# One square root batch for the first two chunks, and another hand-written order of every queue

## The chip, the cores and the metric

The kernel runs on one core of a Trainium2 chip. The metric is the time of one execution on the device in microseconds; several executions are made and their median is taken.

## The reference

Two layers in a row, on x of shape (4, 6336, 256), that is 25344 tokens of 256 features:

```python
# first layer: a gated linear recurrence over the tokens of each batch
a_t  = exp(8 * sigmoid(r_gate) * log(clip(sigmoid(a_param))))
norm = sqrt(max(1 - a_t * a_t, 1e-6))
x_gated = norm * sigmoid(i_gate) * x
for t in range(S):
    h = a_t[:, t] * h + x_gated[:, t]
    y[:, t] = h
# second layer, on y: a causal convolution of 5 taps per feature makes a gate
gate = sigmoid(sum_k conv_w[k] * shifted(y, k))
out  = (gate * (y @ w_val)) @ w_out
```

All inputs and the output are float32 in device memory: r, i and x are read (78 MB) and the output is written (26 MB).

## The kernel before

The tokens are cut into 51 *windows* of 256 or 512 tokens, and the windows into 28 *chunks*: chunk 0 and 1 are one window of 256 each, chunk 2 one of 512, chunks 3 to 25 two windows of 512 each, chunk 26 one of 512, chunk 27 one of 256. So chunk c from 3 on holds windows 2c-3 and 2c-2. Every step is a small function `op_xx`, and the list `ORDER` names the steps one after the other with their chunk or window (and half h of the 256 features), and after an @ the PSUM banks. Each engine takes its own instructions in the order of that list; a step waits on its engine until its inputs are there and its buffer is free, and everything later on that engine waits behind it. No scheduler moves anything.

The life of a chunk, by the names of the steps:

- `lr`, `li`, `lx` (w): SyncE issues the load of a window's r, i or x into rings of four windows each (`NRI`, `NII`, `NX`), so a load of window w can only be issued when the window four earlier has been read. All loads and all stores stand in the one queue of SyncE.
- `ta` (c), `tb` (c): ScalarE, tanh of r/2 and of i/2 (the sigmoids). `pp`, `up` (w): GpSimd, tanh + 1, then times x; for windows 1, 2 and 6 TensorE brings x into PSUM (`xp`) and VectorE does both (`uv`).
- `tr` (c, h): TensorE transposes the tanh of r, `ex` (c, h): ScalarE takes the exponential into `aring` (the decay a, features on the partitions; chunks paired by `GROUPS`). `sq` (c, h): GpSimd squares a (`sa`: ScalarE does).
- `rt` (b): ScalarE takes sqrt(0.25 - 0.25 a^2) over all chunks of batch b of `BATCHES`, into `ering`. The square root needs another table than tanh and exp, so going there and back costs two table loads (line 529).
- `nt` (c): TensorE transposes the roots, `xg` (c): VectorE multiplies them into u, `xt` (c): TensorE transposes the product, `sc` (c, h): VectorE runs the recurrence as one scan per half into `yring`.
- `cv` (w): TensorE convolution, `tg`: ScalarE tanh of it, `vl`: TensorE y @ w_val, `gv`: VectorE product of the two, `ou`: TensorE product with w_out, `cd` or `ca`: copy of the result from PSUM to `oring` (four slots, `NOSB`) by VectorE or by ScalarE, `st`: SyncE issues the store.
- `s_wl` (k): the four loads of the weights, `s_wcast`: GpSimd casts them.

The lines of the profile: L188 and L529 table loads, L289 loads, L307 ta, L310 tb, L317 pp, L329 up, L334 xp, L343 uv, L354 tr, L370 ex, L378 sq, L397 rt, L412 nt, L419 xg, L428 xt, L450 sc, L462 cv, L469 tg, L477 vl, L482 gv, L492 ou, L500 cd, L502 ca, L513 st.

Two places that words don't give as well, the root over a batch, and the walk over the list with its table loads:

```python
            while k < len(cs):
                m = k + 1
                while m < len(cs) and e_at[cs[m]] == e_at[cs[m - 1]] + clen[cs[m - 1]]:
                    m += 1
                o = e_at[cs[k]]
                n = e_at[cs[m - 1]] + clen[cs[m - 1]] - o
                nc.scalar.activation(...)   # Sqrt over 2 * n columns
        ...
        table, have = {"ta": EXP, "tb": EXP, "tg": EXP, "ex": EXP, "rt": SQRT}, EXP
        for word in ORDER.split():
            ...
            if table.get(name, have) != have:
                have = table[name]
                nc.scalar.preload_act_table_set(have)
            emit[name](...)
```

Of the kernel before, what the change touches and what calls it, by code (L numbers as in the profile page):

```python
# [16 lines left out]
CHUNKS = [[256], [256], [512], [512, 512], [512, 512], [512, 512], [512, 512], [512, 512], [512, 512], [512, 512], [512,  # L17
    512], [512, 512], [512, 512], [512, 512], [512, 512], [512, 512], [512, 512], [512, 512], [512, 512], [512,
    512], [512, 512], [512, 512], [512, 512], [512, 512], [512, 512], [512, 512], [512], [256]]
BATCHES = [[0], [1], [2], [3, 4], [5, 6, 7], [8, 9, 10], [11, 12, 13], [14, 15, 16], [17, 18, 19], [20, 21, 22], [23, 24,  # L20
    25], [26, 27]]
# [12 lines left out]
GROUPS = [[0], [1], [2], [3, 4], [5, 6], [7, 8], [9, 10], [11], [12], [13, 14], [15, 16], [17, 18], [19, 20], [21], [22],  # L34
    [23, 24], [25], [26], [27]]
# [7 lines left out]
tr.5.0@6,7 ex.5.0 xt.1@5,4 li.9 lr.13 sc.0.0 sc.0.1 pp.3 up.4 lx.8 nt.3@2,3 xt.2@0,1 sc.1.0 li.10 up.3 sc.1.1 xg.3  # L43
xt.3@2,3 tb.5 cv.1@4,5 sc.2.1 lx.7 sc.2.0 tg.1 cv.0@6,7 tg.0 tr.5.1@0,1 ex.5.1 s_wcast vl.1@4,5 sc.3.1 sc.3.0 xp.6@6,7
vl.0@0,1 nt.4@2,3 li.12 pp.5 ta.7 lr.16 sq.5.0 sq.6.0 up.5 li.11 ta.8 pp.8 uv.6 tb.6 gv.0 ou.0.0@0 lr.15 cv.2@6,7 tg.2
xg.4 tr.7.1@2,3 ex.7.1 cd.0.0 xt.4@1,0 st.0 gv.1 ou.1.0@4 cd.1.0 pp.7 tr.7.0@6,7 vl.2@4,5 ex.7.0 lx.10 sc.4.1 gv.2
cv.3@2,3 ou.2.0@4,5 vl.4@6,7 st.1 up.8 li.14 lr.18 up.7 sq.6.1 tb.7 lx.9 cd.2.0 tg.3 cv.4@2,3 ta.9 vl.3@4,5 lr.17
sc.4.0 cv.6@0,1 tg.4 gv.4 gv.3 ou.3.0@4,5 sq.7.1 st.2 sq.7.0 lr.20 sq.5.1 pp.12 ou.4.0@6,7 cd.4.0 rt.4 lx.11 li.13
lx.12 lr.19 pp.10 cd.3.0 up.10 st.3 st.4 cv.5@2,3 nt.5@4,5 tg.5 tg.6 xg.5 nt.6@6,7 pp.9 up.9 xg.6 lx.14 li.16 li.15
ta.10 lr.21 lr.22 xt.5@4,5 tb.8 lx.13 sq.8.1 pp.11 ta.11 lr.24 lr.23 vl.5@0,1 tr.9.1@6,7 sc.5.1 ex.9.1 sc.5.0 gv.5  # L50
xt.6@2,3 sc.6.0 tr.9.0@4,5 ex.9.0 vl.6@0,1 li.18 cv.7@6,7 li.17 gv.6 nt.7@4,5 up.11 up.12 tb.9 cv.8@0,1 tg.7 sc.6.1
ta.12 xg.7 ou.5.0@6,7 cd.5.0 tg.8 ou.6.0@2,3 li.20 lx.16 cv.9@4,5 cd.6.0 xt.7@0,1 pp.14 up.14 sq.9.1 pp.13 st.5
vl.7@2,3 sq.9.0 up.13 sc.7.0 ta.13 lx.15 tg.9 tb.10 st.6 li.19 lx.17 tr.12.1@6 vl.9@4,5 gv.7 gv.9 ou.7.0@2,3 cd.7.0
sq.10.1 ou.9.0@4,5 sc.7.1 cd.9.0 cv.10@2,3 lr.25 sq.10.0 sq.8.0 rt.5 pp.17 lr.26 st.7 vl.8@0,1 tr.12.0@7 gv.8 pp.16
# [49 lines left out]
def kernel(  # L104
# [456 lines left out]
```

## Time and profile before

| what | us |
|---|---|
| median of 3 runs | 296.16 (295.24 to 296.34) |
| the profiled execution | 295.84 |
| its span, first to last instruction | 293.7 |
| ScalarE (ACT) busy | 276.1 (94%) |
| VectorE (DVE) busy | 243.4 (83%) |
| GpSimd (POOL) busy | 241.8 (82%) |
| TensorE (PE) busy | 237.7 (81%) |
| SyncE's DMA queue, share of 16 engines' span | 92.6%, 104.35 MB |

An engine's busy time is the sum of its instructions, without overlap. A row of a group gives the line, the engine, the operation, the tile written and those read, shapes, the count, then busy time and mean ns of one, then idle time of the engine before such instructions and what ended it. A window gives busy time of each engine in a stretch, with the share of the DMA engines and the rate they moved. The times of single instructions on ScalarE and VectorE overlap the next by about 0.1 us: 0.9 us from start to start for a 1.0 us instruction.

### The profile page before, as it was taken

How to read it: one execution, taken by the hardware profiler on the slowest of the kernel's cores; microseconds unless marked ns; L12 is line 12 of the kernel's file. 1: busy time of each engine (PE TensorE's matmuls, PEld its weight loads, DVE VectorE, ACT ScalarE, POOL GpSimd, SP SyncE). 2: the span in 40 equal slices, each digit the busy share in tenths (PEclk: the TensorE clock that was granted, in tenths of full speed). 3: DMA queues.
4: the chain of work that ended last, by engine and by line, in shares of the span. 5: the costliest groups of instructions: out<-in, count | busy, mean ns of one | idle time of the engine just before them, and what ended most of it. 6: DMA issues, size and time to landing. Idle time of an engine off the chain costs nothing.

```text
span 293.7 us, 6223 instructions
## 1 busy us (share of the span) xinstructions
PE 237.7 (81%) x2470; PEld 163.7 (56%) x2497; DVE 243.4 (83%) x211; ACT 276.1 (94%) x200; POOL 241.8 (82%) x161
## 2 busy tenths in 40 slices
PE   2263778777697899997969889888889998999993
PEld 1241555445364758566636657556648664767652
DVE  5000797857999899998999998999999999999981
ACT  4899999999999999999999999999999999999754
POOL 1559979999899979999998899999998999565300
PEclk9996899999999999999999999999999999999999
DMA  7899999999999999999998999999999999965336
GB/s 240 310 405 389 382 407 408 413 407 383 402 405 389 394 367 407 394 379 396 413 330 286 370 415 413 421 363 408 378 374 387 381 345 374 352 224 214 148 144 250
DMA packets 29995, 104.75 MB, mean 357 GB/s; under 512 B 3335, under 2 KB 3854, under 8 KB 29966
## 3 DMA queue, kind: packets, MB, share of 16 engines
q1 hardware_dynamic: 29952, 104.35, 92.6%
q8 instruction: 19, 0.31, 0.4%
q14 instruction: 10, 0.08, 0.1%
q10 hardware_dynamic: 14, 0.01, 0.0%
HBM read 78.39 MB, written 25.95 MB: 355 GB/s over the span
## 4 chain that ended last, share of the span: by engine, by line
ACT 33%; PE 20%; DMA 19%; issue 11%; DVE 9%; POOL 3%; SPq 2%; ACTq 0%; DVEq 0%; POOLq 0%
DMA xring<-in_x_dram 10%; ACT ering L397 7%; ACT aring L370 6%; ACT tgring L469 6%; ACT tbring L310 6%; PE banks L477 5%; DMA rring<-in_r_gate_dram 5%; PE banks L492 5%; PE banks L462 4%; ACT taring L307 3%; ACT L529 3%; DVE tgring L482 3%; PE banks L412 3%; DMA out_dram<-oring 3%; DVE oring L500 2%
## 5 line engine op out<-in xcount | busy, mean ns | idle before, releaser
L329 POOL TENSOR_TENSOR uring<-tbring,xring 128x1024 bf16<-128x1024 bf16 (+1 forms) x48 | 100.8, 2114 | 9.2 <-DMA xring<-in_x_dram 8.3
L450 DVE TENSOR_TENSOR_SCAN yring<-aring,yring,banks 128x1024 bf16<-128x1024 f32 (+5 forms) x54 | 106.1, 1988 | 2.1 <-PE banks L428 1.9
L378 POOL TENSOR_TENSOR ering<-aring 128x1024 f32<-128x1024 f32 (+2 forms) x54 | 91.4, 1712 | 10.5 <-ACT aring L370 10.5
L462 PE MATMUL banks<-yring,diag 64*64 64x512 bf16 (+7 forms) x1080 | 62.0, 361 | 4.0 <-ACT tgring L469 1.4
L482 DVE SCALAR_TENSOR_TENSOR tgring<-tgring,banks 128x1024 bf16<-128x1024 bf16 (+1 forms) x51 | 58.9, 1177 | 6.1 <-ACT tgring L469 4.5
L317 POOL TENSOR_SCALAR tbring<-tbring 128x1024 bf16<-128x1024 bf16 (+1 forms) x48 | 48.8, 1028 | 12.2 <-ACT tbring L310 11.9
L492 PE MATMUL banks<-wo,tgring 128*128 128x256 bf16 x396 | 51.1, 274 | 7.3 <-DVE tgring L482 6.3
L370 ACT ACTIVATE aring<-banks,khf 128x2048 f32<-128x2048 bf16 (+3 forms) x38 | 54.4, 1469 | 0.6 <-PE banks L354 0.6
L477 PE MATMUL banks<-yring,wv 128*128 128x512 bf16 (+7 forms) x189 | 47.9, 358 | 6.2 <-ACT tgring L469 2.2
L469 ACT ACTIVATE tgring<-banks 128x1024 bf16<-128x1024 f32 (+1 forms) x51 | 49.6, 1004 | 3.2 <-PE banks L462 3.0
L492 PEld LDWEIGHTS <-tgring 128*128 128x128 bf16 x396 | 41.5, 114 | 17.7 <-DVE tgring L482 12.5
L310 ACT ACTIVATE tbring<-iring 128x2048 bf16<-128x2048 f32 (+2 forms) x28 | 48.1, 1718 | 3.2 <-DMA iring<-in_i_gate_dram 3.2
L307 ACT ACTIVATE taring<-rring 128x2048 bf16<-128x2048 f32 (+2 forms) x28 | 48.0, 1721 | 1.8 <-DMA rring<-in_r_gate_dram 1.7
L397 ACT ACTIVATE ering<-ering 128x4096 bf16<-128x4096 f32 (+5 forms) x15 | 44.7, 3017 | 0.1
L462 PEld LDWEIGHTS <-diag 64*64 64x64 bf16 x1080 | 28.8, 106 | 27.8 <-issue 11.6
L354 PE MATMUL banks<-ident_b,taring 128*128 128x128 bf16 x396 | 30.1, 230 | 16.4 <-ACT taring L307 8.7
L419 DVE TENSOR_TENSOR uring<-banks,uring 128x2048 bf16<-128x2048 bf16 (+2 forms) x28 | 30.3, 1093 | 15.3 <-PE banks L412 14.0
L500 DVE COPY oring<-banks 128x1024 f32<-128x1024 f32 (+1 forms) x33 | 38.2, 1180 | 5.2 <-PE banks L492 5.1
L354 PEld LDWEIGHTS <-taring 128*128 128x128 bf16 x396 | 26.1, 103 | 22.1 <-issue 10.2
L477 PEld LDWEIGHTS <-wv 128*128 128x128 bf16 x216 | 19.5, 97 | 25.9 <-issue 12.6
L412 PE MATMUL banks<-ident,ering 128*128 128x128 f32 x198 | 29.1, 290 | 5.7 <-ACT ering L397 3.2
L412 PEld LDWEIGHTS banks<-ident,ering 128*128 128x128 f32 x198 | 26.0, 207 | 11.2 <-ACT ering L397 6.0
(43 smaller groups left out, 126.3 us busy)
## 6 DMA issues: line engine op xcount, KB each, us to landing
rring<-in_r_gate_dram SPq DMA_DIRECT2D x48, 512.0 KB, 7.8
iring<-in_i_gate_dram SPq DMA_DIRECT2D x48, 512.0 KB, 7.2
xring<-in_x_dram SPq DMA_DIRECT2D x48, 512.0 KB, 7.7
out_dram<-oring SPq DMA_DIRECT2D x48, 512.0 KB, 5.1
rring<-in_r_gate_dram SPq DMA_DIRECT2D x3, 256.0 KB, 3.0
iring<-in_i_gate_dram SPq DMA_DIRECT2D x3, 256.0 KB, 5.4
xring<-in_x_dram SPq DMA_DIRECT2D x3, 256.0 KB, 5.1
out_dram<-oring SPq DMA_DIRECT2D x3, 256.0 KB, 6.4
```

The source lines that it names most:

```text
L310: nc.scalar.activation(**tangent(c, tbring, NTI, iring, NII))
L329: nc.gpsimd.tensor_tensor(out=u, in0=t1, in1=xt, op=ALU.mult)
L370: nc.scalar.activation(out=dst, in_=src, func=ACT.Exp, scale=khf[:, h:h + 1], bias=khf[:, h:h + 1])
L378: nc.gpsimd.tensor_tensor(out=e, in0=a, in1=a, op=ALU.mult)
L397: nc.scalar.activation(out=ering[:].bitcast(BF16)[:, 4 * o:4 * o + 2 * n], in_=ering[:, 2 * o:2 * o + 2 * n], func=ACT.Sqrt, scale=-0.25, ...
L412: nc.tensor.transpose(out=bank[:, k:k + P], in_=ering[:, e + q:e + wins[w] // 2:nq], identity=ident[:])
L450: nc.vector.tensor_tensor_scan(out=yring[:, h, col:col + o1 - o0], data0=aring[:, h, a_at[c] + o0:a_at[c] + o1], data1=xT[:, o0:o1], initi ...
L462: nc.tensor.matmul(out=gp[oh * 64:oh * 64 + 64, h, a:b], lhsT=diag[half * 64:half * 64 + 64, h, k, :], rhs=yring[half * 64:half * 64 + 64, ...
L469: nc.scalar.activation(out=tgring[:, w % NTG, :, 0:wins[w]], in_=live.pop(("gp", w))[:, :, 0:wins[w]], func=ACT.Tanh, scale=0.5)
L477: nc.tensor.matmul(out=val[:, m, a:b], lhsT=wv[:, hk, m * P:(m + 1) * P], rhs=yring[:, hk, col:col + b - a], start=(hk == 0), stop=(hk == ...
L482: nc.vector.scalar_tensor_tensor(out=tgring[:, w % NTG, :, 0:wins[w]], in0=tgring[:, w % NTG, :, 0:wins[w]], scalar=1.0, in1=live.pop(("va ...
L492: nc.tensor.matmul(out=ops[:, j * D:(j + 1) * D], lhsT=gv[:, hk, j:wins[w]:J], rhs=wo[:, hk, :], start=(hk == 0), stop=(hk == H - 1))
```

## The change

`BATCHES` starts with `[0, 1], [2]` in place of `[0], [1], [2]`, so the roots of chunks 0 and 1 are one instruction, and there are 11 batches numbered 0 to 10 in place of 12. The batches from `[3, 4]` on hold the same chunks, with a number less by one. `ORDER` is another list: the same steps in another order for all five queues, other PSUM banks, and four of the 18 ScalarE copies of results (`ca`) are VectorE copies (`cd`) in it. `CHUNKS` and `GROUPS` are the same lists with other line breaks. Nothing else is changed; all lines of the file move down by one.

```diff
-BATCHES = [[0], [1], [2], [3, 4], [5, 6, 7], [8, 9, 10], [11, 12, 13], [14, 15, 16], [17, 18, 19], [20, 21, 22], [23, 24,
-    25], [26, 27]]
+BATCHES = [[0, 1], [2], [3, 4], [5, 6, 7], [8, 9, 10], [11, 12, 13], [14, 15, 16], [17, 18, 19], [20, 21, 22], [23,
+    24, 25], [26, 27]]
...
-s_ident s_small s_kt s_diag lr.0 ta.0 lr.1 ta.1 li.0 tr.0.1@0 tb.0 pp.0 tr.0.0@1 ex.0.1 tr.1.0@2 tr.1.1@3 lr.2 ta.2
-ex.1.0 tr.2.1@0 ex.1.1 ex.2.1 tr.2.0@2 lr.3 lr.4 lr.5 ex.0.0 ta.3 lr.6 ta.4 li.1 tr.3.1@0,1 lx.1 tb.1 sq.2.1 sq.1.1
-sq.0.1 ex.2.0 li.2 tr.3.0@2,3 li.4 lx.0 li.3 tb.2 xp.1@4 sq.0.0 sq.1.0 sq.2.0 up.0 uv.1 lr.7 lr.8 ex.3.1 sq.4.1 ex.3.0
-sq.3.0 lr.9 lr.10 lx.2 lx.4 s_wl.2 lx.3 li.5 li.6 s_wl.1 tb.3 s_wl.3 s_wl.0 ta.5 lx.5 ta.6 lr.14 rt.0 xp.2@2,3 nt.0@4
-xg.0 xt.0@0,1 li.8 li.7 uv.2 rt.1 rt.2 nt.1@4 nt.2@5 xg.2 xg.1 pp.4 sq.3.1 sq.4.0 lx.6 rt.3 lr.11 tb.4 lr.12
...
+s_ident s_small s_kt s_diag lr.1 lr.0 s_wl.3 s_wl.2 lr.2 lr.3 ta.0 ta.1 lr.4 lr.5 tr.0.0@0 ta.2 lr.6 tr.0.1@1
+tr.1.0@2 tr.2.0@3 ex.0.1 ex.0.0 tr.2.1@4 tr.1.1@5 ex.1.1 li.0 lx.0 ex.1.0 li.2 ex.2.1 ta.3 sq.0.1 lr.8 lr.7 ex.2.0
+ta.4 sq.1.1 tb.0 s_wl.0 lr.10 tr.3.1@2,3 tb.2 lr.9 sq.2.1 pp.0 up.0 sq.0.0 li.4 tr.3.0@4,5 ex.3.1 ex.3.0 li.3 li.1
+lx.2 ta.5 lx.4 sq.4.1 lx.1 sq.2.0 sq.3.1 ta.6 lr.13 lr.12 sq.4.0 tb.3 tr.5.0@4,5 li.6 pp.4 sq.3.0 tb.1 li.7 xp.2@2,3
+s_wl.1 lx.3 ex.5.0 li.5 sq.1.0 lx.6 uv.2 up.4 xp.1@0 rt.0 uv.1 rt.1 sq.5.0 tr.5.1@4,5 nt.1@0 nt.0@1 lr.14 rt.2 xg.0
+xg.1 li.8 nt.2@2 xt.0@6,7 lr.11 xg.2 sc.0.1 xt.2@2,3 xt.1@0,1 sc.0.0 lx.5 s_wcast sc.1.0 sc.1.1 cv.1@0,1 nt.3@6,7
+pp.3 tb.4 li.9 sc.2.0 sc.2.1 up.3 xp.6@2,3 ex.5.1 lx.8 pp.5 xg.3 uv.6 li.10 ta.8 tg.1 sq.5.1 cv.0@4,5 xt.3@6,7
+sc.3.0 vl.0@2,3 vl.1@0,1 gv.1 tg.0 up.5 sq.6.1 ta.7 tr.7.0@4,5 lr.18 nt.4@0,1 lx.10 lr.15 lr.17 gv.0 tb.5 ou.1.0@6
+sc.3.1 tr.7.1@2,3 ex.7.0 lx.7 li.12 xg.4 ou.0.0@7 sq.6.0 ex.7.1 cd.0.0 cv.3@4,5 li.11 xt.4@0,1 pp.7 pp.8 cd.1.0 st.1
+tg.3 cv.4@2,3 sq.7.1 tb.6 vl.2@4,5 sq.7.0 sc.4.0 cv.2@6,7 tg.4 sc.4.1 li.13 st.0 lx.9 vl.3@2,3 up.7 pp.9 up.8 tg.2
+li.14 gv.2 vl.4@6,7 rt.3 sq.8.0 gv.4 ou.2.0@4,5 cv.5@0,1 cd.2.0 ou.4.0@6,7 gv.3 st.2 lx.12 cv.6@4,5 cd.4.0
+ou.3.0@2,3 pp.10 sq.8.1 st.4 lr.16 nt.5@6,7 cd.3.0 up.9 up.10 tg.5 xg.5 st.3 vl.5@2,3 lx.11 ta.10 gv.5 xt.5@6,7
...
+ou.38.0@4,5 sc.22.0 cv.40@2,3 pp.43 up.43 pp.44 ou.37.0@6,7 cd.38.0 cd.37.0 st.38 lx.45 vl.39@4,5 vl.40@6,7 li.48
+sc.22.1 st.37 up.44 li.47 lx.47 lr.49 rt.9 lr.50 gv.39 nt.23@0,1 pp.45 cv.41@4,5 up.46 tg.40 xg.23 vl.41@2,3 gv.40
...
+up.49 vl.45@4,5 sc.25.1 st.43 tg.46 gv.45 lx.50 vl.46@6,7 ou.44.0@2,3 rt.10 cv.47@0,1 gv.46 up.50 ca.44.0 nt.26@4
+nt.27@5 tg.47 ou.45.0@6,7 xg.26 st.44 xg.27 xt.26@2,3 cd.45.0 cv.48@4,5 sc.26.1 sc.26.0 st.45 ou.46.0@6,7 tg.48
+vl.47@0,1 ca.46.0 vl.48@4,5 st.46 gv.47 cv.49@2,3 gv.48 ou.47.0@0,1 tg.49 xt.27@4,5 sc.27.0 ca.47.0 vl.49@6,7
+sc.27.1 ou.48.0@2,3 st.47 gv.49 cv.50@4,5 ca.48.0 vl.50@0,1 tg.50 st.48 ou.49.0@6,7 gv.50 ca.49.0 ou.50.0@0 ca.50.0
+st.49 st.50
```

The part of the old list that ends it, from its last square root batch (26, 27) on:

```
ou.42.0@4,5 tg.44 rt.11 st.41 lx.49 nt.25@6,7 ca.42.0 gv.43 vl.44@0,1 xg.25 ou.43.0@2,3 xt.25@6,7 ca.43.0 gv.44
cv.46@4,5 tb.27 tg.46 cv.45@2,3 tg.45 sc.25.1 sc.25.0 st.42 ou.44.0@0,1 ca.44.0 nt.26@7 st.43 st.44 up.49 xg.26
vl.46@4,5 gv.46 vl.45@2,3 gv.45 cv.47@0,1 tg.47 ou.46.0@4,5 ca.46.0 xt.26@6,7 sc.26.0 ou.45.0@0,1 vl.47@2,3 ca.45.0
...
```

More of the change, by code (lines that the diff above doesn't have):

```diff
@@ L33 @@
 LOG_TERMS = [15, 13, 11, 9, 7, 5, 3]
[L34 to L35 removed]
+GROUPS = [[0], [1], [2], [3, 4], [5, 6], [7, 8], [9, 10], [11], [12], [13, 14], [15, 16], [17, 18], [19, 20], [21],
+    [22], [23, 24], [25], [26], [27]]
 ORDER = """
[L38 to L39 removed]
@@ new lines @@
+li.20 xt.7@4,5 cd.7.0 pp.13 pp.16 ou.9.0@2,3 sc.7.0 st.7 up.13 lx.15 li.19 cd.9.0 up.14 sc.7.1 st.9 lx.18 tg.10
+vl.10@0,1 nt.8@2,3 up.16 tr.12.0@4 lr.25 lx.17 lr.26 ta.11 cv.11@6,7 xg.8 gv.10 xt.8@2,3 ex.12.0 up.15 ou.10.0@0,1
+sc.8.0 tg.11 cv.12@4,5 tb.10 sq.12.0 vl.11@6,7 cd.10.0 tg.12 tr.12.1@2 gv.11 pp.17 ex.12.1 st.10 tr.11.1@0 lr.23
+lr.24 pp.18 sc.8.1 tb.11 lx.19 li.22 vl.12@4,5 tr.11.0@1 nt.9@6,7 lx.20 up.18 ex.11.1 xg.9 ou.11.0@2,3 xt.9@6,7
+gv.12 cd.11.0 up.17 ta.14 ex.11.0 cv.14@4,5 st.11 li.21 li.23 cv.13@2,3 li.24 sc.9.1 pp.20 sq.12.1 pp.19 ta.13
@@ new lines @@
+sc.9.0 tr.13.1@0,1 lr.30 sq.11.0 tg.14 lx.21 lx.22 tg.13 vl.13@4,5 ex.13.1 tr.13.0@2,3 gv.13 up.19 vl.14@6,7 ex.13.0
+nt.10@4,5 gv.14 up.20 ou.13.0@0,1 xg.10 ou.12.0@6,7 tb.12 cd.13.0 xt.10@4,5 sq.13.0 cv.16@2,3 cd.12.0 st.13 tb.13
+lr.28 cv.15@0,1 sc.10.1 st.12 lr.27 tg.16 li.25 vl.15@6,7 tg.15 sq.13.1 sq.11.1 vl.16@2,3 sc.10.0 ou.14.0@0,1 rt.5
+cd.14.0 cv.17@4,5 cv.18@0,1 pp.23 pp.22 pp.21 gv.15 st.14 up.21 lr.29 lx.23 gv.16 ou.15.0@6,7 ou.16.0@2,3 cd.15.0
+cd.16.0 st.15 nt.11@6,7 tg.17 li.26 sq.14.1 st.16 vl.17@2,3 lx.24 xg.11 li.28 pp.24 sq.14.0 up.22 li.27 gv.17
@@ new lines @@
+xt.11@6,7 nt.12@4,5 ta.15 ta.16 tg.18 ou.17.0@2,3 sc.11.1 sc.11.0 up.23 lr.33 lr.34 tr.15.0@0,1 tb.14 xg.12
+tr.15.1@6,7 ex.15.0 cd.17.0 vl.18@4,5 up.24 st.17 xt.12@2,3 gv.18 lr.31 lx.25 ex.15.1 cv.20@0,1 sc.12.0 li.29
+sq.15.0 lx.28 vl.19@4,5 cv.19@6,7 tb.15 sc.12.1 sq.16.1 tg.20 pp.27 ou.18.0@0,1 cd.18.0 tg.19 ta.18 cv.21@2,3 gv.19
+st.18 vl.20@6,7 lx.26 lr.32 tg.21 sq.16.0 sq.15.1 li.30 lx.27 nt.13@0,1 gv.20 ou.19.0@2,3 xg.13 pp.26 vl.21@6,7
+ou.20.0@4,5 cd.19.0 pp.28 gv.21 xt.13@0,1 pp.25 up.25 cd.20.0 rt.6 ou.21.0@6,7 cv.22@2,3 st.20 lr.37 st.19 vl.22@4,5
@@ new lines @@
+up.28 lr.38 sc.13.0 sc.13.1 tg.22 up.26 ta.17 nt.14@2,3 gv.22 nt.15@0,1 up.27 tb.16 lr.35 tr.17.1@4,5 xg.14 cd.21.0
+st.21 tr.17.0@2,3 ex.17.1 lr.36 lx.29 xg.15 xt.14@6,7 li.31 li.32 lx.30 ex.17.0 cv.23@4,5 pp.29 sq.18.1 vl.23@0,1
+tg.23 sc.14.0 ou.22.0@2,3 cv.24@4,5 ta.20 gv.23 sc.14.1 ou.23.0@0,1 ca.22.0 tg.24 xt.15@2,3 sq.17.0 cd.23.0 ta.19
+cv.26@6,7 sq.18.0 st.22 up.29 li.33 sc.15.1 st.23 cv.25@0,1 li.34 tg.26 lr.39 pp.30 tr.19.1@4,5 tg.25 sc.15.0
+vl.24@6,7 gv.24 tb.17 up.30 lr.40 nt.16@0,1 ex.19.1 tr.19.0@2,3 sq.17.1 xg.16 ou.24.0@6,7 ex.19.0 sq.20.1 cd.24.0
@@ new lines @@
+xt.16@0,1 cv.27@4,5 sc.16.0 st.24 tb.18 lx.32 sq.20.0 sq.19.1 sq.19.0 vl.25@2,3 lx.31 lx.33 cv.28@6,7 tg.27 gv.25
+ta.21 sc.16.1 ou.25.0@2,3 vl.28@4,5 tg.28 pp.34 pp.32 pp.31 cd.25.0 vl.27@0,1 vl.26@6,7 gv.28 li.36 st.25 lx.34 rt.7
+up.32 lr.42 lr.41 gv.26 ou.28.0@4,5 gv.27 ou.26.0@6,7 cd.26.0 up.31 cd.28.0 st.26 cv.29@2,3 li.35 ou.27.0@0,1 li.38
+nt.17@6,7 cd.27.0 li.37 up.34 pp.33 lx.36 tr.21.0@4 xg.17 tg.29 vl.29@0,1 lr.44 ex.21.0 xt.17@6,7 gv.29 ta.22
+vl.30@2,3 tr.21.1@0 cv.30@4,5 ex.21.1 lr.43 lx.35 lr.46 lr.45 tg.30 nt.18@0,1 sc.17.1 sc.17.0 up.33 sq.21.1 tb.19
@@ new lines @@
+xg.20 lx.41 ex.23.0 tr.23.1@0,1 gv.35 up.40 pp.39 ou.33.0@2,3 ex.23.1 xt.20@4,5 up.39 cd.33.0 nt.21@6,7 sc.20.1
+xg.21 st.33 cv.36@2,3 tb.22 lx.42 sq.24.0 tg.36 li.45 pp.42 li.46 vl.36@0,1 ta.25 li.44 li.43 ou.34.0@2,3 sc.20.0
+sq.24.1 pp.41 xt.21@6,7 tr.25.1@5 ca.34.0 gv.36 ex.25.1 tr.25.0@4 st.34 up.41 ou.35.0@2,3 ex.25.0 sc.21.0 cv.37@0,1
+up.42 ca.35.0 st.35 sc.21.1 cv.38@4,5 vl.37@2,3 lx.43 tg.37 sq.23.1 sq.23.0 sa.25.1 nt.22@0,1 gv.37 tg.38 tb.24
+ou.36.0@6,7 sq.25.0 xg.22 vl.38@4,5 tb.23 cd.36.0 cv.39@2,3 gv.38 st.36 xt.22@0,1 pp.46 tg.39 lx.44 lx.46
```

77 lines of the change are left out of this document (17 added, 60 removed).

## The prediction

> **What bounds the kernel now.** I read the page's busy times first, then the stretches between the square root batches, then the timelines of ScalarE and VectorE, the groups by form, and the chain.
>
> ```profile
> PE 237.7 (81%) x2470; PEld 163.7 (56%) x2497; DVE 243.4 (83%) x211; ACT 276.1 (94%) x200; POOL 241.8 (82%) x161
> 0.00:62.29 62.29, 36.99 (x327) 23.55 (x329) 30.76 (x49) 55.93 (x44) 46.21 (x42) 0.95 0.97 372
> 62.29:267.21 204.92, 178.96 (x1917) 125.79 (x1940) 194.17 (x146) 203.00 (x138) 191.66 (x117) 1.00 0.98 375
> 267.21:293.70 26.49, 21.80 (x229) 14.40 (x230) 18.46 (x18) 17.13 (x18) 3.95 (x3) 1.00 0.45 181
> ```
>
> The last three lines are stretches (length; PE, PEld, DVE, ACT, POOL; clock, DMA share, GB/s), cut where rt.4 (62.29) and the last batch, rt.11 (267.21), begin. Between them ScalarE works 203.0 of 204.9 us, VectorE 194.2 and the transfers 98%: ScalarE sets the pace, the other two are close behind. After rt.11 nobody is full but TensorE (21.8 of 26.5).
>
> ```profile
> 31.18 0.42 DVE L419 TENSOR_TENSOR uring<-banks,uring 128x512 bf16<-128x512 bf16 x1 [9.22 <-PE banks L412]
> ...
> 61.01 2.35 DVE L482 SCALAR_TENSOR_TENSOR tgring<-tgring,banks 128x1024 bf16<-128x1024 bf16 x2 [1.42 <-ACT tgring L469]
> 65.40 2.36 DVE L500 COPY oring<-banks 128x1024 f32<-128x1024 f32 x2 [2.03 <-PE banks L492]
> 69.21 2.35 DVE L419 TENSOR_TENSOR uring<-banks,uring 128x2048 bf16<-128x2048 bf16 x2 [1.45 <-PE banks L412]
> ...
> 176.97 1.23 DVE L419 TENSOR_TENSOR uring<-banks,uring 128x2048 bf16<-128x2048 bf16 x1 [1.23 <-PE banks L412]
> ...
> 274.72 0.67 DVE L419 TENSOR_TENSOR uring<-banks,uring 128x1024 bf16<-128x1024 bf16 x1
> ```
>
> VectorE's timeline: it starts on xg.0 at 31.18, begins xg.5 at 69.21 and xg.26 at 274.72. Its listed waits between the last two sum to 7.2 us, most of them for roots that ScalarE had not made.
>
> ```profile
> L502 ACT COPY oring<-banks 128x1024 f32<-128x1024 f32 x17 | 17.3, 1021 | 3.0 <-PE banks L492 2.3 <-DMA out_dram<-oring 0.7
> L397 ACT ACTIVATE ering<-ering 128x512 bf16<-128x512 f32 x2 | 1.2, 622 | 0.0
> L397 ACT ACTIVATE ering<-ering 128x1024 bf16<-128x1024 f32 x1 | 1.0, 1041 | 0.0
> L500 DVE COPY oring<-banks 128x1024 f32<-128x1024 f32 x31 | 36.8, 1212 | 3.3 <-PE banks L492 3.2
> ```
>
> These price the copies and the joint root; start to start, the steps take on ScalarE 0.90 (ca), 0.94 (tg), 1.80 (ta, tb), 1.95 (ex), 0.53 (256-token tb, ex), on VectorE 1.13 (cd, gv), 2.25 (sc).
>
> **The joint batch and the opening.** It saves 2 x 0.622 - 1.041 = 0.2 us of ScalarE. It saves no table load: walking the new list gives 18 switches, as the old one (18 loads of 1.283 us). What counts is when each batch starts. Replay of ScalarE in the new list: ta.2 needs lr.2, which stands behind 1.18 MB instead of 1.31 (li.0 out of the way, 0.13 MB of weights in), so about 7.9 instead of 8.46. Then five ex, ta.3, ex.2.0 fill it to 14.5; ta.4 found lr.6 at 14.30 before and needs it no earlier. From 14.5: ta.4, tb.0, tb.2, two ex, ta.5, ta.6 = 1.80 + 0.53 + 0.95 + 3.90 + 3.60 = 10.8, to 25.3; tb.3 needs 7.73 MB of the queue, and lx.2, at 8.39 MB, landed at 26.89 before, so I take 26.0; tb.3, tb.1, ex.5.0 and the load (1.80 + 0.53 + 1.95 + 1.28) end at 31.7. There rt.0 starts, against 28.94, with ex.5.0 done ahead. GpSimd must have sq.1.0 by then: pp.4 after tb.3 (27.8), sq.3.0, sq.1.0, 1.04 + 1.89 + 0.61, ends at 31.4: just in time. xg.0 moves from 31.18 to about 33.8. GpSimd then does up.4, sq.5.0, the weight casts (2.3), pp.3 and up.3, to 40.9, so xg.3 starts at 41.0 instead of 36.40: a loss on VectorE here.
>
> ScalarE from 31.7: roots of chunks 0 to 4 (1.04 + 1.04 + 3.6), load, then 5 tanh of 1.80, 3 ex of 1.95, 2 + 3 tg, load: rt.3 (chunks 5 to 7) begins at **58.8**, 3.5 us before rt.4 did, because the list has one ta and one tb less ahead of it. VectorE from xg.3: 1.1 xg, 1.4 uv.6, four scans, xg.4, five gv, five copies (all counted, with 1 to 2 us of waits) reach 65.1; the roots are ready at 64.1, nt.5 at 65.1: xg.5 begins at **65.2**, 4.0 us earlier than 69.21. Before xg.5 the two lists hold exactly the same VectorE steps, so this is a true lead.
>
> **The long middle.** ScalarE from rt.3 to rt.10 has, against rt.4 to rt.11: one copy less, one ta, one 512-window-pair tb, one small tb and two tg more: -0.90 + 1.80 + 1.80 + 0.53 + 1.88 = +5.1. At its old idle of 1.9 us, rt.10 begins at 58.8 + 204.9 + 5.1 = **268.8**, xg.26 2.1 later (root 1.5, two nt): 270.9. VectorE from xg.5 to xg.26 has three copies and two gv more: 5 x 1.13 = 5.65. With its old waits: 65.2 + 205.5 + 5.65 = **276.4**; with all 7.2 us of waits gone, 269.2. The four copies are thus free on ScalarE's line and cost 4.5 us on VectorE's, where the cover is the old waits; without that cover they cost the whole 4.5. The two lines lie so close that neither waits for the other by the old amount: I take xg.26 at 273.2, half a microsecond under the middle of 270.9 and 276.4, since ScalarE's old waits were few.
>
> At this place the Trainium skill speaks against the change: "Perfetto Trace Analysis", Optimizing Scalar/DVE Operations, says that where VectorE is full, work should go to ScalarE, and the change does the reverse. The trace agrees as far as VectorE is 96% busy from 69.21 to 274.72 (197.9 of 205.5), but ScalarE is 99% (203.6). By that rule the result is rival B.
>
> **The transfers.** No bytes are added. By 62.29 about 23.2 MB had moved (372 GB/s x 62.29). tb.25 and ta.27 need 94.9 and 96.2 MB of the new queue, at about 246 and 251 us on ScalarE's line. At the 392 GB/s of the stretch 62.29 to 140 these are through at 245 and 248.5, at the mean of 375 at 253.5 and 257: no slack in the first case, 6 to 7 us late in the second. What lowers the mean is mainly one stretch:
>
> ```profile
> 62.29:140.00 77.71, 64.98 (x688) 46.54 (x696) 70.80 (x54) 77.56 (x49) 74.56 (x45) 1.00 1.01 392
> 140.00:160.00 20.00, 16.84 (x169) 10.56 (x170) 19.74 (x15) 19.94 (x12) 19.13 (x12) 1.00 0.92 346
> ```
>
> There lr.40 stood 5.2 us in SyncE's queue for ta.19, which stood behind rt.7 on ScalarE. In the new list the batch of the same chunks (rt.6) has st.20, lr.37, st.19 and lr.38 right behind it, whose slots are free by then: 2.1 MB, 5.4 us of transfers under a root of 5.3. Also, ca.23 follows the store that frees its slot of `oring` (st.19) with no ScalarE work between and waited 0.67 us; in the new list 4.1 us or more lie between every such pair. I take 1 to 2 us for late transfers, within the 273.2.
>
> **The tail.** After the last batch begins, the new list has three copies, two tg and one tb less on ScalarE and TensorE 14.2 us (by the rows 1.15 cv, 0.87 vl, 0.9 ou) against 21.8. Following it from xg.26: xg.27, cd.45, two scans of 1.2 to 4.9; cv.49, ou.47, xt.27, vl.49, gv.49 to 10.3; ou.49, ca.49, ou.50, ca.50 to 13.1; store 3.0 (ca.50 ended at 290.7, span 293.7): 16.1, and 17.8 if VectorE waits as much as before. I take 17.1. Before it was 19.0.
>
> **Sum.** 273.2 + 17.1 = 290.3 us of span. The profiled execution took 295.84, 2.14 beyond its span, and the median of the runs is 0.32 above it: 290.3 + 2.5 = **292.8**.
>
> **The rivals.**
> - A, the forecast: both lines meet, xg.26 between 271 (with the short tail) and 275: 289.6 to 294.6. Chance 0.50.
> - D: ScalarE's line alone decides, VectorE loses all its waits: 270.9 + 16.1 = 287.0, so 289.5. For it: the old waits were for ScalarE. Against: xg.3's 4.6 us delay, and two full engines seldom mesh. 0.08.
> - B: VectorE is the bound and keeps its waits: 276.4 + 17.1 = 293.5, so 296.0, no change. For it: waits for nt and tg recur at every batch. Against: in the new list VectorE has three to five gv, copies or scans queued behind each of rt.3 to rt.8, before the xg that needs it; in the old one a single copy or gv stood there behind rt.4 and rt.5. 0.19.
> - C, slower: the transfers become the bound. Loads wait in SyncE's queue behind stores, stores behind copies on a late VectorE, so the queue runs dry as in 140 to 160. At 375 GB/s ta.27 comes 6 us late, with one or two more such stretches (1.6 us each, 8% of 20) 8 to 10: xg.26 at 278.5 to 281, 298.1 to 300.6. It decides from xg.26 later than 278, a middle stretch under about 375 GB/s. For it: three resources at 96 to 99%. Against: the weak stretch had its cause in an order that the new list does not repeat. 0.23. The Trainium skill, "DMA: Bandwidth & Descriptors", Specifications, gives 358 GB/s as the limit of a core's device memory; by it ta.27 would come at 266, 15 us late, and the time be near 305 us. The trace disagrees: 392 GB/s over 78 us.
> - That the joint batch saves a pair of loads is excluded by the count.
>
> **How the numbers follow.** About 0.5% (1.5 us) is what a measurement of this kernel can tell from no change: faster is under 294.7, slower over 297.6. A and D are faster, 0.58; B is the same, 0.19; C is slower, 0.23. The range goes from D's lower edge, 289, into C until half of it is out, 299.5. The faster cases alone: 289 to 294.6.
>
> **What would show it.** Right: rt.3 near 58.8 and xg.5 near 65.2; the last root near 270; VectorE's waits between xg.5 and xg.26 down from 7.2 to 3 or 4 us; from xg.26 to the end 16 to 18 us; no stretch with a DMA share under 0.95 before 240. Wrong: rt.0 after 33 (the opening), ScalarE waiting for rring or iring for over 3 us in the middle (C), or VectorE's waits at 7 us again (B).

## The result, and the profile after

The changed kernel takes 298.8 us in the median of 20 runs (295.18 to 303.95), the kernel before 296.07 (293.97 to 297.99). The ratio is 1.0054, 95% interval 1.0029 to 1.008: slower, by just over the 0.5% that can be told from no change. (Executions more than 1.5% above a kernel's fastest are left out of every ratio here, so ratios can be smaller than quotients of medians.) The forecast was 292.8 and faster. The profiled execution took 298.79, with a span of 297.0. Its span is 3.3 us longer than the one before, twice the 1.6 us that the ratio gives, so the account of it below adds up to more than the typical loss. The new times also spread wider, over 8.8 us against 4.0.

The first view is the page's busy line, then the stretches of the new kernel, cut where rt.3 (58.89) and the last batch, rt.10 (277.19), begin. Columns as in the prediction: length; PE, PEld, DVE, ACT, POOL busy; clock, DMA share, GB/s.

```profile
PE 245.6 (83%) x2472; PEld 167.5 (56%) x2497; DVE 248.4 (84%) x215; ACT 274.0 (92%) x195; POOL 242.2 (82%) x161
```

```profile
0.00:58.89 58.89, 36.23 (x301) 23.71 (x302) 28.81 (x47) 52.30 (x42) 42.22 (x39) 0.97 0.97 363
58.89:277.19 218.30, 194.79 (x2020) 134.41 (x2044) 208.14 (x156) 209.98 (x143) 198.66 (x122) 0.98 0.97 365
277.19:297.00 19.81, 14.57 (x154) 9.34 (x153) 11.48 (x14) 11.69 (x12) 1.35 (x2) 0.93 0.47 186
```

The opening is 3.4 us shorter (58.89 against 62.29), the tail 6.7 shorter (19.81 against 26.49), the middle 13.4 longer (218.30 against 204.92): the sum is the 3.3 us between the spans. In the middle ScalarE worked 7.0 us more than before and stood idle 8.3 us (218.30 - 209.98) in place of 1.9.

VectorE's timeline, its first step of xg.5 and that of xg.26:

```profile
65.53 1.21 DVE L420 TENSOR_TENSOR uring<-banks,uring 128x2048 bf16<-128x2048 bf16 x1
...
279.58 0.69 DVE L420 TENSOR_TENSOR uring<-banks,uring 128x1024 bf16<-128x1024 bf16 x1 [1.08 <-PE banks L413]
```

Between these VectorE was busy 203.75 us (197.87 before) and idle 10.3 (before 7.6). From xg.26 to the end it took 17.4 us (before 19.0). So on VectorE's path: 3.7 us of lead, then +5.9 of work and +2.7 of waits, then 1.6 gained: +3.3.

What ScalarE waited for in the middle, from the list of its waits (engine, tile, line <- releaser: us in all, times, longest):

```profile
ACT tbring L311 <- DMA iring<-in_i_gate_dram: 3.2, 5, 0.8
ACT oring L503 <- PE banks L493: 1.7, 1, 1.7
ACT tgring L470 <- PE banks L463: 1.2, 4, 0.4
ACT aring L371 <- PE banks L355: 1.0, 2, 0.6
ACT taring L308 <- DMA rring<-in_r_gate_dram: 0.2, 1, 0.2
```

Loads of i and r are 3.4 us of the 8.3, TensorE's results 3.9. SyncE's own waits at stores in the middle, before (62.29 to 267.21) and after (58.89 to 277.19), show what can make loads late:

```profile
SPq L513 <- DVE oring L500: 55.3, 19, 5.3
SPq L513 <- ACT oring L502: 22.1, 6, 6.5
```

```profile
SPq L514 <- DVE oring L501: 82.4, 29, 5.9
SPq L514 <- ACT oring L503: 22.2, 8, 7.0
```

SyncE stands 104.6 us at stores whose copies aren't made yet, against 77.4. Every load listed behind such a store waits with it. SyncE's timeline shows how (start, length of the issue):

```profile
71.18 0.33 SPq L290 DMA_DIRECT2D iring<-in_i_gate_dram  x1
73.73 0.34 SPq L514 DMA_DIRECT2D out_dram<-oring  x1
74.13 1.39 SPq L290 DMA_DIRECT2D iring<-in_i_gate_dram  x2
75.57 1.09 SPq L290 DMA_DIRECT2D rring<-in_r_gate_dram  x1
79.36 0.34 SPq L514 DMA_DIRECT2D out_dram<-oring  x1
79.76 0.42 SPq L290 DMA_DIRECT2D rring<-in_r_gate_dram  x1
```

Two stores hold the queue for 2.2 us (71.51 to 73.73) and 2.7 us (76.66 to 79.36); each time loads go out at once behind. What is issued and not yet moved averages 1.24 MB in the middle (1.36 before; my count from the trace's issues and packets). Stretches of the new kernel fall below the old one's, which holds 392 GB/s from 62.29 to 140 and 391 from 160 to 220 (its row first, then the new kernel's):

```profile
160.00:220.00 60.00, 52.98 (x572) 36.63 (x579) 57.17 (x44) 58.98 (x41) 57.79 (x36) 1.00 1.02 391
```

```profile
58.89:140.00 81.11, 69.64 (x726) 50.39 (x734) 76.71 (x59) 78.56 (x49) 76.18 (x47) 0.96 1.00 382
140.00:160.00 20.00, 18.00 (x166) 11.68 (x168) 18.86 (x14) 19.88 (x13) 19.92 (x13) 0.99 0.95 357
160.00:220.00 60.00, 54.45 (x593) 36.64 (x598) 57.84 (x45) 58.72 (x39) 54.20 (x33) 1.00 1.00 382
```

A third thing that the old trace did not have in its middle: TensorE's clock fell to half for 3.41 us at 92.7, 137.1 and 222.4.

```profile
92.70:96.10 3.40, 3.40 (x28) 2.65 (x31) 3.40 (x3) 3.39 (x4) 2.60 (x2) 0.50 0.91 331
137.10:140.50 3.40, 3.22 (x28) 2.90 (x27) 3.06 (x3) 3.40 (x2) 1.05 (x1) 0.50 1.00 404
222.40:225.80 3.40, 3.18 (x13) 2.30 (x13) 2.28 (x2) 3.39 (x3) 3.32 (x3) 0.50 1.03 420
```

### The profile page after: what moved, and what is told of

Its sections match the earlier page's. It is cut to its first block, busy times and chain, and to the rows that moved or that the text cites. A ratio compares the mean times of both kernels' runs of the same rounds, so it can differ in the third digit from the quotient of the medians.

```text
span 297.0 us, 6228 instructions
## 1 busy us (share of the span) xinstructions
PE 245.6 (83%) x2472; PEld 167.5 (56%) x2497; DVE 248.4 (84%) x215; ACT 274.0 (92%) x195; POOL 242.2 (82%) x161
## 4 chain that ended last, share of the span: by engine, by line
PE 28%; DMA 22%; ACT 17%; DVE 13%; issue 10%; POOL 4%; SPq 4%; ACTq 0%; DVEq 0%; POOLq 0%
DMA xring<-in_x_dram 10%; DVE yring L451 8%; PE banks L463 8%; DMA iring<-in_i_gate_dram 8%; PE banks L493 6%; PE banks L413 5%; PE banks L478 4%; DMA rring<-in_r_gate_dram 4%; ACT aring L371 4%; ACT taring L308 3%; SPq L290 3%; POOL ering L379 3%; ACT tgring L470 3%; DVE oring L501 3%; ACT ering L398 3%
## 5 line engine op out<-in xcount | busy, mean ns | idle before, releaser
L463 PE MATMUL banks<-yring,diag 64*64 64x512 bf16 (+7 forms) x1080 | 65.3, 366 | 6.8 <-DVE yring L451 6.4
L470 ACT ACTIVATE tgring<-banks 128x1024 bf16<-128x1024 f32 (+1 forms) x51 | 50.5, 1000 | 4.5 <-PE banks L463 4.0
L493 PE MATMUL banks<-wo,tgring 128*128 128x256 bf16 x396 | 51.9, 274 | 2.8 <-DVE tgring L483 2.1
L478 PE MATMUL banks<-yring,wv 128*128 128x512 bf16 (+7 forms) x191 | 49.9, 364 | 3.8 <-ACT tgring L470 1.5
L355 PE MATMUL banks<-ident_b,taring 128*128 128x128 bf16 x396 | 32.6, 242 | 19.3 <-ACT taring L308 15.5
L501 DVE COPY oring<-banks 128x1024 f32<-128x1024 f32 (+1 forms) x37 | 43.4, 1186 | 2.6 <-PE banks L493 1.4
L398 ACT ACTIVATE ering<-ering 128x4096 bf16<-128x4096 f32 (+4 forms) x14 | 44.6, 3217 | 0.1
L355 PEld LDWEIGHTS <-taring 128*128 128x128 bf16 x396 | 28.0, 109 | 26.1 <-ACT taring L308 17.9
L413 PE MATMUL banks<-ident,ering 128*128 128x128 f32 x198 | 31.1, 305 | 6.4 <-DVE oring L501 2.4
L413 PEld LDWEIGHTS banks<-ident,ering 128*128 128x128 f32 x198 | 27.4, 208 | 11.9 <-ACT ering L398 5.8
```

Of the source, the lines that this page charges most:

```text
L355: nc.tensor.transpose(out=bank[:, o:o + P], in_=taring[:, place(w, NTR), j, h * P:(h + 1) * P], identity=ident_b[:])
L413: nc.tensor.transpose(out=bank[:, k:k + P], in_=ering[:, e + q:e + wins[w] // 2:nq], identity=ident[:])
L463: nc.tensor.matmul(out=gp[oh * 64:oh * 64 + 64, h, a:b], lhsT=diag[half * 64:half * 64 + 64, h, k, :], rhs=yring[half * 64:half * 64 + 64, ...
L470: nc.scalar.activation(out=tgring[:, w % NTG, :, 0:wins[w]], in_=live.pop(("gp", w))[:, :, 0:wins[w]], func=ACT.Tanh, scale=0.5)
L478: nc.tensor.matmul(out=val[:, m, a:b], lhsT=wv[:, hk, m * P:(m + 1) * P], rhs=yring[:, hk, col:col + b - a], start=(hk == 0), stop=(hk == ...
L493: nc.tensor.matmul(out=ops[:, j * D:(j + 1) * D], lhsT=gv[:, hk, j:wins[w]:J], rhs=wo[:, hk, :], start=(hk == 0), stop=(hk == H - 1))
```

## The experiments

Four theories, by the letters that the expectations use. T: loads are late because they stand in SyncE's one queue behind stores of late copies (rival C of the prediction). V: VectorE, with four copies more, is the bound (rival B). P: TensorE is, by its half-clock spells or its load. S: ScalarE alone. All ratios are to the kernel before, in five rounds, with their 95% interval; the change itself is at 1.0054 [1.0029, 1.008].

**The copies, in each list.** In the new list five VectorE copies go to ScalarE and one the other way, so that the engines of the copies are those of the old list (the four named at the change are the net of these); in the old list the reverse.

```diff
 new list:  -cd.8.0  cd.21.0 ca.22.0 cd.23.0 cd.33.0 cd.45.0
            +ca.8.0  ca.21.0 cd.22.0 ca.23.0 ca.33.0 ca.45.0
 old list:  the same six, the other way
```

New list: 

> The changed order with every result copied by the engine that copied it before (windows 8, 21, 23, 33, 45 back to ScalarE, 22 to VectorE): VectorE has 4.5 us less, ScalarE 4.1 more. Theory V (VectorE is the bound, rival B): 3 to 4.5 us faster than the changed kernel, about 293.5 to 295. Theory T (transfers come late) and theory P (TensorE, with its half-clock spells, holds the others up): ScalarE's extra work adds to the loss, 299 to 301.

Old list: 

> The old order with the copies of the new one (windows 8, 21, 23, 33, 45 on VectorE, 22 on ScalarE), nothing else. ScalarE, 99% busy in the middle, is freed of 4.1 us. If ScalarE alone sets the old pace: 292 to 293. Theory V: VectorE takes over, within 1 us of before or up to 3 us slower. Theories T and P: 294 to 296, since what ScalarE gains is lost to other waits.

Measured: 301.41, ratio 1.0172 [1.0128, 1.0217], and 302.29, ratio 1.0211 [1.0168, 1.0255]. Both are slower, the second by more than any of the theories gave. In the new list VectorE has less to do and the time grows; in the old list ScalarE is relieved (201.25 us busy in the middle, 203.00 before) and stands idle 9.7 us there. The copies are not what costs the new list its time: V as the only bound falls, S too. Each list fits its own copies only; through which waits the exchange costs so much was not followed up.

**Fewer bytes.** From window 8 on half of each x window is not loaded (a result from old data in that half of the ring), in the new list and in the old one as a control; then, in another pair, half of each output window is not stored. Either takes 11 MB off the queue.

```diff
+            if which == "x" and w >= 8:
+                dst, src = dst[:, 0:J // 2, :], src[:, 0:J // 2, :]
 ...
 other pair, in the store, with 0:m in place of 0:J:
+            m = J // 2 if w >= 8 else J
 ...
```

New list, half of x: 

> The changed kernel with half of each x window left unloaded from window 8 on (11 MB of 104 less; the steps compute on what the slot held). Theory T: ScalarE's waits for iring and rring go, 3 to 6 us faster than the changed kernel, 291.5 to 294.5. Theories V and P: at most 1.5 us faster, 296 or more.

Old list, half of x: 

> Control for the run with half of x: the old order with half of each x window left unloaded from window 8 on. Theory T (the new order alone is short of transfers): the old order gains at most 1 us, 295 or more. If transfers hold both orders alike, it gains as much as the new one did, 3 to 4 us, about 292.5, and late transfers don't explain the difference between the orders.

New list, half of the output: 

> The changed kernel with half of each output window left unwritten from window 8 on (11 MB less, the same as in the run with half of x, but from the stores). Theory T (all transfers together are short): as fast as that run, 293 to 295. If it was x itself that GpSimd had waited for: at most 1.5 us faster than the changed kernel, 296 or more.

Old list, half of the output: 

> Control: the old order with half of each output window left unwritten from window 8 on. Theory T: at most 1.5 us faster than before (294.5 or more), against 4 us in the new order. If all transfers cost both orders alike: 291.5 to 293.

Measured, new and old: half of x 294.27, 0.9933 [0.9905, 0.9961], and 294.91, 0.9962 [0.9938, 0.9986]; half of the output 293.81, 0.9914 [0.9883, 0.9946], and 294.4, 0.9945 [0.9915, 0.9975]. The new list gains 1.2% and 1.4%, the old one 0.4% and 0.6%. The middle of the new list with half of x:

```profile
58.37:272.51 214.14, 192.53 (x2020) 133.38 (x2044) 207.48 (x156) 209.09 (x142) 199.55 (x123) 0.98 0.89 322
```

ScalarE's idle time is down from 8.3 to 5.0 us (214.14 - 209.09). So waiting for transfers costs the new list at least 3.6 to 4.1 us (1.0054 less the ratio, times 296), the old one 1.1 to 1.6. The difference, 2.5 us, covers the 1.6 that the change lost. This bears out T as to the transfers. It doesn't yet say that the order of the queue is at fault.

**Loads ahead of stores.** In SyncE's order 97 loads move ahead of one or two stores, wherever the slot that they fill is free by then; nothing else moves. One place of the queue, as it was and as it is:

```diff
-lr.33 lr.34 st.17 lr.31 lx.25 li.29 lx.28 st.18 lx.26 lr.32 li.30 lx.27 st.20 lr.37 st.19 lr.38
+lr.33 lr.34 lr.31 lx.25 li.29 lx.28 lx.26 lr.32 li.30 lx.27 st.17 lr.37 st.18 lr.38 st.20 st.19
```

> The changed kernel with the loads moved ahead of up to two stores in SyncE's queue wherever their slot is free by then in the list (97 loads move; no other queue changes). Theory T by the mechanism of rival C (loads stand behind stores that wait for late copies): ScalarE's and GpSimd's waits for loads go down from 7.6 and 8.7 us, 2 to 4 us faster, 294 to 296. If the transfers are late because the queue is full, not because it is blocked: no gain, or slower by waits of the copies for their slots of oring, 297 to 300.

Measured: 300.91, ratio 1.0182 [1.0143, 1.0222], a miss. The queue was fuller (1.60 MB in the mean against 1.24, by the same count), but stores left later, and now copies waited for a slot of the four in `oring`, on full engines:

```profile
DVE oring L498 <- DMA out_dram<-oring: 5.3, 2, 3.1
...
ACT oring L500 <- DMA out_dram<-oring: 1.7, 1, 1.7
```

In the old list the only such wait was the 0.67 us of ca.23, and the changed kernel has none. Does the move help once the copies have room? Six slots in `oring`, the memory taken from the u ring, ten slots to six. Then the control with the slots alone, and the old list with 88 of its loads moved by the same rule and the same slots.

```diff
-NU = 10
+NU = 6
-NOSB = 4
+NOSB = 6
```

New list, loads ahead, six slots: 

> The run with the loads ahead of the stores again, with six slots of oring instead of four, so that a late store holds up no copy. If that run lost by copies that waited for their slots (5.3 us of VectorE): back to the changed kernel or better, 295 to 298. If stores and loads share a full queue whichever goes first: still 299 or more.

New list, six slots alone: 

> The changed list, no step moved, with six slots of oring instead of four (room from the ring of u): tells whether the gain of the run with loads ahead and six slots came from the slots alone. If the stores' place ahead of the loads is the cause: no gain, within 1 us of the changed kernel, 297 to 298.5. If the slots alone were short: 294 to 295.

Old list, loads ahead, six slots: 

> The same remedy on the old order: loads ahead of up to two stores (88 move), six slots of oring. If the old order was short of nothing (ScalarE idle 1.9 us in its middle): within 1 us of before, 295 to 297. If the queue's order costs both alike: 292.5 to 294, and it would be no part of the difference between the two orders.

Measured: 294.02, 0.9944 [0.9915, 0.9974]; 298.76, 1.0025 [0.9981, 1.007]; 294.75, 0.9949 [0.9921, 0.9977]. The first is the fastest whole computation of the study, under both kernels. Its middle (rt.3 to rt.10) and the stretch 160 to 220, the waits of SyncE in the middle, and xg.26 on VectorE:

```profile
58.61:271.58 212.97, 192.59 (x2043) 132.34 (x2044) 207.34 (x156) 208.85 (x143) 199.92 (x124) 0.99 0.97 375
160.00:220.00 60.00, 54.71 (x592) 36.40 (x590) 58.53 (x45) 59.88 (x40) 56.56 (x35) 1.00 1.02 403
```

```profile
SPq L287 <- POOL uring L327: 33.7, 14, 5.4
SPq L287 <- ACT taring L305: 20.3, 7, 7.0
SPq L511 <- ACT oring L500: 16.9, 5, 7.0
...
SPq L511 <- DVE oring L498: 11.4, 5, 4.6
```

```profile
273.97 0.69 DVE L417 TENSOR_TENSOR uring<-banks,uring 128x1024 bf16<-128x1024 bf16 x1 [0.54 <-PE banks L410]
```

SyncE stands 28.3 us at stores in place of 104.6; the stretch 160 to 220 moves 403 GB/s in place of 382; ScalarE's idle time is 4.1 us (212.97 - 208.85) and xg.26 starts at 273.97, where the forecast had 273.2. The span is 291.4: of the 5.6 us gained, 5.3 lie in the middle (4.2 of idle time, 1.1 of work). SyncE does not stand less in all: its listed waits in the middle sum to 121.2 us before, 131.5 after the change and 145.7 here. What counts is where it stands. At a load whose slot is still being read (the two L287 rows) the loads are as far ahead as their rings allow; at a store, loads with free slots wait behind it. Neither half does it alone: loads ahead without slots lose, and slots without loads ahead show no clear gain. The expectation for the old list missed: its queue too had 0.5% to give (the old list with the slots alone was not run). With the queue mended the two lists are level (0.9944 and 0.9949).

**More slots for the loads.** Rings of six windows for i, then for r, in the new list.

```diff
-NU = 10
+NU = 6
-NII = 4        other kernel: -NRI = 4
+NII = 6                      +NRI = 6
```

i: 

> The same with six slots for i. The waits of ScalarE for i (4.1 us in the profile of the changed kernel) should go if they come from blocked slots: 294.5 to 296. If the queue waits for the stores' copies: 297 to 298.5.

r: 

> The changed list with six slots for r instead of four (room from the ring of u, ten slots to six; no step moves). SyncE waits less for slots, so its queue runs on. Theory T, by the blocked queue: SyncE's 17.6 us of waits for ta go down to under 5, 2 to 3 us faster than the changed kernel, 294.5 to 296. If the queue waits for the stores' copies instead (122 us of waits in the profile of the changed kernel): within 1 us of the changed kernel, 297 to 298.5.

Measured: 298.05, 1.0069 [1.0031, 1.0108]: more slots for i bring nothing, so it is not they that hold the loads back. With six windows of r 320.53, 1.0772 [1.0703, 1.0842], where ScalarE waited 26.8 us for r. That run does not test the slots: the list has the loads of r for windows 21, 22, 25, 26, 37 and 38 ahead of the tanh of the windows six earlier, whose slots they take in a ring of six, so those `ta` are listed behind loads that overwrite their r, and the output is another. Nothing is concluded from it.

**The clock of TensorE.** Some matmuls of the identity with itself, their results not used, fill the gaps ahead of the half-clock spells: six places in the new list, five in the old one as a control. And in the new list one of the five taps of the convolution is left out, a lighter TensorE.

```diff
+        def op_wm(n, *at):
+            for _ in range(n):
+                nc.tensor.matmul(out=banks[:, at[0], 0:P], lhsT=ident_b[:], rhs=ident_b[:], start=True, stop=True)
 the list, one of the places:
-nt.8@2,3
+wm.20@2 nt.8@2,3
 the other kernel:
-                for k in range(CONV_K):
+                for k in range(1, CONV_K):
 ...
-                                             start=(k == 0), stop=(k == CONV_K - 1))
+                                             start=(k == 1), stop=(k == CONV_K - 1))
```

Filled, new list: 

> The changed kernel with 10 to 20 small matmuls without use (1 us or less) put on TensorE ahead of six steps for which it stood idle 1 to 2 us (windows' cv.7, cv.35, nt.8, nt.23, tr.13, tr.15). Theory P: no half-clock spells in the middle, mean clock 0.985 or more, 2 to 4 us faster than the changed kernel, 294 to 296. Theories V and T: clock up, time within 1 us of the changed kernel, about 297.5.

Filled, old list: 

> Control for the run with matmuls without use: the old order with 10 to 20 of them ahead of five steps for which TensorE stood idle (nt.5, tr.9, tr.15, nt.17, nt.23). Theory P (half-clock spells cost the new order more): no gain here, within 1 us of before, as its profiled execution had no spell after 31 us. If spells come and go in both orders by chance: 1 to 2 us faster, 294 to 295.

A tap less, new list: 

> The changed kernel with 4 of the 5 taps of the convolution (the first left out): TensorE has some 12 us of 246 less, no other engine changes. Theory P: 3 to 6 us faster than the changed kernel, 292 to 295. Theory V (VectorE itself is the bound and waits for nobody that matters): at most 1.5 us faster. Theory T: the same, at most 1.5.

Measured: 296.89, 1.0004 [0.9965, 1.0043]; 297.63, 1.0062 [1.0034, 1.009]; 298.11, 1.0059 [1.0022, 1.0096]. With one spell left of three the new list may have gained 0.5%, but the interval overlaps that of the change. The old list, with no spell to lose in its middle, became 0.6% slower, a miss, so the fillers may have a price of their own that hides a gain: not settled. A lighter TensorE gains nothing, at a lower mean clock (0.963 against 0.977 in the changed kernel, over the runs in the ratios): P, as load, falls.

**Which part of the list.** Three kernels that change over from one list to the other, banks of steps across the joint renamed: at xg.5 from new to old, at xg.5 from old to new, and at the root of chunks 23 to 25 from old to new.

```diff
 ORDER = new list up to xg.5          + what is left, in the old list's order
 ORDER = old list up to xg.5          + what is left, in the new list's order
 ORDER = old list up to that root     + what is left, in the new list's order
```

> The new list up to xg.5, with the joint batch, then every step that is left in the order of the old list, copies on the old engines. If the new opening's lead of VectorE (3.7 us) is worth something by itself and only the new middle loses: 292 to 294. If ScalarE sets the pace (theory S: at xg.5 the new list has one ta and one tb less behind it, 3.6 us that ScalarE still owes): no change, 295.5 to 296.5. Theory T: 295 to 297, as the old middle keeps its transfers fed.

> The old list up to xg.5, then every step that is left in the order of the new list. If the loss is made in the new middle (theories T and P): slower than before, 297 to 300. If it comes from the opening's state handed on (fewer tanh done by 58.9 us, fewer bytes moved), it goes away here: 293 to 295.5.

> The old list up to the root of chunks 23 to 25, then what is left in the order of the new list. The new profile needs 1.6 us less from xg.26 to the end, the old one 5 us less between the last two roots. If the shorter end is the order's own: 294 to 295. If it only mirrors what had been done before it: 295.5 to 297.

Measured: 303.0, 1.0221 [1.0182, 1.026]; 301.6, 1.0169 [1.0122, 1.0215]; 298.74, 1.0085 [1.0049, 1.012]. All three missed what was expected of them. The first two are slower than either list and the third is level with the new one (the intervals overlap), so the place of the loss can't be read from them: a joint can starve somebody by itself. The stretch behind the first joint, and what ScalarE waited for in it:

```profile
58.94:98.05 39.11, 27.34 (x258) 19.34 (x259) 28.40 (x21) 33.09 (x21) 32.96 (x21) 0.91 0.88 334
```

```profile
ACT taring L305 <- DMA rring<-in_r_gate_dram: 6.0, 3, 2.6
```

ScalarE loses 6.0 us there (39.11 - 33.09) at 334 GB/s, all of it at loads of r. It shows only what loads that come late once can cost: more than the whole change was to bring.

## Why the prediction was wrong

- **The opening** was right: rt.0 at 31.47 (31.7 forecast), rt.3 at 58.89 (58.8), xg.5 at 65.53 (65.2). The replay of ScalarE and GpSimd held (xg.0 at 34.00 for 33.8, xg.3 at 41.39 for 41.0), and the lead was real.
- **The tail** was right: 17.4 us from xg.26 to the end (17.1).
- **VectorE's work** was right: +5.9 us between xg.5 and xg.26 (5.65). **ScalarE's work** came out at +7.0 where 5.1 was forecast. Summed by groups its instructions grew by 4.5; the rest is overlap of one instruction with the next (10.6 us in all before, 8.1 now), lost where it stops and starts.
- **The step that failed** is "I take xg.26 at 273.2": it began at 279.58. Both lines were to meet with less waiting than VectorE's old one, since VectorE had more queued to do. Its listed waits were to fall from 7.2 to 3 or 4 us, and they rose to 9.6; ScalarE's idle time rose from 1.9 to 8.3, where 273.2 had room for about 4. On ScalarE's line this gives the whole delay: rt.10 came at 277.19 in place of 268.8, by 6.4 us of idle time and 1.9 of work (0.1 was there at rt.3).
- **The mis-sized term** in it is "1 to 2 us for late transfers, within the 273.2". By the runs it is at least 3.6 to 4.1 us on the path. I had checked the one weak stretch of the old trace and found its cause gone. But SyncE's waits at stores were in the old trace at 77.4 us already; I did not price them. In the new list it is 37 waits in place of 25, 104.6 us. The mechanism is that of rival C as written: loads behind stores, stores behind copies. Its signs came: 3.4 us of ScalarE's waits for i and r in the middle (over 3), the middle at 365 GB/s (under 375), xg.26 at 279.58 (in its 278.5 to 281). The size that C gave, 298.1 to 300.6, holds the median of 298.8, but partly by luck: C put all of the delay down to transfers, and they were part of it. The runs with fewer bytes and the run with loads ahead and six slots show the mechanism; of the controls only the old list's slots alone are missing.
- **A second part of the same step** was not late transfers. Between the last two roots ScalarE waits 3.6 us in the changed kernel (0.7 of it for a load of i, the rest mostly for TensorE's results), and 3.05 to 3.14 in seven others with the new list, those with half of x, with half of the output and with loads ahead and six slots among them (there it is 3.07 of the 4.1 us left in the middle). With six windows of i it is 5.13, with the old list 0.66. The stretch before and after:

```profile
244.88:267.21 22.33, 20.89 (x216) 14.84 (x220) 22.28 (x16) 21.67 (x19) 16.65 (x12) 1.00 0.83 308
```

```profile
246.39:277.19 30.80, 29.02 (x283) 18.61 (x280) 30.30 (x21) 27.17 (x26) 23.51 (x17) 1.00 0.87 307
```

  VectorE is full in both, with 22.28 of 22.33 and 30.30 of 30.80 us. But the new list gives it 3.1 us more work there than ScalarE (27.17), the old one 0.6, and TensorE has 29.02. This looks like rival B in one place: "neither waits for the other by the old amount" fails where VectorE has the most to do. No run took work out of that stretch alone, so this is read from the profile and not shown by an experiment.
- **The advice on offloading.** The Trainium skill, "Perfetto Trace Analysis", Optimizing Scalar/DVE Operations, says that offloading some work from a saturated VectorE to ScalarE may make sense. The change did the reverse and was slower, but the runs don't put that down to the copies: moving them back cost another 1.2% (1.0172 against 1.0054).
- **The limit of 358 GB/s.** The Trainium skill, "DMA: Bandwidth & Descriptors", Specifications, gives it for a core's device memory. The trace disagrees again, with 403 GB/s over 60 us with loads ahead and six slots, and the time of about 305 us worked out from it did not come.
- **The comparison.** With the transfers relieved in both, the new list is not the 1.1% faster that was forecast: it is ahead by 0.3% with fewer bytes, within overlapping intervals, and level with loads ahead. The old list had part of the same shortage to give back, and the 3.1 us of waits between the last two roots stay.
- **What stays open:** the price of the half-clock spells. In the runs of the changed kernel that enter the ratio time and mean clock go together (13 runs, correlation -0.56, 0.8 us for 0.01 of clock), but a longer run has more gaps, so either may be the cause. Against a large price: the profiled execution with six windows of i had no such spell in its middle and took 298.37, against 298.79 with three. Nor did any run show which of the 37 late stores cost most.

## What to carry to other kernels

Where one engine sets the pace and two other resources are 96 to 98% full, price the waits between them as growing when the pace-setter is freed, unless the trace shows the slack that is to absorb them. Look at what the queue that issues the transfers stands at, not only at the rate they reach or at how long it stands: a store listed ahead of loads in one in-order queue hands a late copy on to the loads, and moving the loads ahead pays only if the copies have slots enough to let the stores wait. And undo a suspected cost in the kernel before as well: half of what a relief brings may be there to be had in both.

## What the runs showed of the hardware

- TensorE's clock halved for 3.41 us after gaps of only 1.84 to 1.98 us in the changed kernel (90.49 to 92.47, 134.67 to 136.66, 219.43 to 221.27). Within each trace all such spells start on a grid of 3.413 us. Gaps as long did nothing elsewhere: 2.01 us at 74.32 in the kernel before, 2.03 at 70.61 in the new one. In these two kernels, between 34 us and TensorE's last instruction, a spell came behind each step of the grid that was 55 to 60% idle, and none behind a step at 47% or less. This is no threshold: in the run with filled gaps one step 58% idle had no spell behind it.
- The rate of the transfers goes down when little is pending. Over stretches of 10 us in four traces (both kernels, and loads ahead with four and with six slots) it was 335 GB/s in the mean of the 20 with less than 1 MB issued and not yet moved (229 to 395), and 404 in the mean of the 25 with 2 MB or more (362 to 418).
- Removing a fifth of the convolution's matmuls lowered the mean clock, 0.977 to 0.963 over the runs in the ratios, and did not shorten the run (1.0059 against 1.0054).
